# A kernel of mLSTM chunks and a soft mixture of experts on one core: gates, decays and last steps in another order, and the output taken in parts of 128 and 192 columns

## The chip, the cores and the metric

The kernel runs on one core of a Trainium2 chip. The metric is the device time of one execution in microseconds (us). The profile used below is of one execution by the hardware profiler; its own time stands beside the times of the runs without it.

## What is computed

The reference has two parts. The first is a gated recurrence over 768 time steps for 4 batches of 8 heads with 40 features; the second takes its output as 3072 tokens of 320 features.

```python
for t in range(S):
    m_new = np.maximum(f_gate[:, :, t] + m, i_gate[:, :, t])
    f_stab = np.exp(f_gate[:, :, t] + m - m_new)
    i_stab = np.exp(i_gate[:, :, t] - m_new)
    C = f_stab[..., None, None] * C + i_stab[..., None, None] * np.einsum('bhd,bhe->bhde', vt, kt)
    n = f_stab[:, :, None] * n + i_stab[:, :, None] * kt
    y[:, :, t] = sigmoid(o_gate) * (C @ qt) / np.maximum(abs(n @ qt), 1.0)
x = y as (3072, 320)
logits = x @ phi                                  # 32 slots
d = softmax of logits over the tokens             # d.T @ x is the input of the slots
slot_out[e] = relu(slot_input[e] @ w1[e]) @ w2[e] # 8 experts, 4 slots each, width 1024
out = (softmax of logits over the slots) @ slot_out
```

## The kernel before

**The chunks.** The recurrence is cut into 24 steps: chunk c = i // 4 (128 time steps each) of batch i % 4. A step is in matrix form. `expo(i)` (L302) makes a matrix of exponents on PE (tile `pe`) and two exponentials on ACT into a slot of `EWt` (3 slots). `scores(i)` (L340) is the 16 matmuls of keys and queries (`psc`), `mix(i)` (L369) multiplies the two on DVE. `pv(i)` (L411) is the product with the values (`ph`, one buffer). `inter(i)` (L352) is the part that comes from the state, scaled on DVE by `inter_ops` into `itt`; `post1` and `post2` (L424, L441) add it, make the denominator and multiply by the output gate; `gate(i)` (L452) multiplies by the reciprocal into x, on POOL up to step 20 and on DVE in the last steps. `xtr(i)` (L460) transposes x on PE and copies it on ACT. `keys`, `state`, `state_dec` and `state_ops` (L374 to L407) bring the state on: keys scaled on POOL, 16 matmuls into `pst`, decay on POOL, addition on DVE.

**The gates.** `gate_part` (L211) is a chain of scans and elementwise operations on DVE and POOL over a stretch of time: columns 0 to 127 before the loop, 128 to 383 as the list `nxt`, the rest a few at a time in `later`. Its results in `Y` are brought into the operands of `expo` by `side(i)` (ACT, `LLt`) and `spread(i)` (DVE, `RRt`), together `chunk_ops(i)` (L285). `last_sums` and `decays(c)` (L319, L328) make the decays of a chunk: a transpose on PE into the tile `pg`, an exponential on ACT (`eg`), a small matmul into other columns of the same tile, a second exponential (`dS`). `pg` is of the tag `pm`, whose two buffers `pi`, `pt`, `pl`, `pd`, `pc` and `psl` also use in turn. It runs in steps 2, 4, 8, 9 and 10.

**The tokens.** Every 4 steps make a group of 512 tokens: logits (`moe_pl`), a running maximum, the sum over the tokens (`moe_dT`, `moe_psl`, `moe_acc`), and the weights over the slots (`moe_e0`, `moe_e`, `comb_s_ops`, `comb_n`, `comb_hi`, `comb_lo`, `comb_T`, `comb_h`).

**The loop** (L694 to L772) runs steps 1 to 20, with the order of each engine's work as it is written; the last three steps and the last two groups are written out from L775 on. Loads are all issued by SP, in order, and wait there until their buffer is free. In step i it issues `load_kv(i + 2)` and `load_qk(i + 3)`, and weights of the experts (`load_w1`, `load_wave`).

**The end.** `up` is the first matmul of the experts, `relu`, `turn` (transposes), and `down(hf, n, rk)` (L940) the second one, for part hf of the 320 columns; each of its 16 pieces for a part is 4 matmuls in fp32. `gather(hf)` brings a part into `so3`, and `combine(hf, q)` (L962), q from 0 to 11, makes two blocks of 128 tokens for that part of the columns: two matmuls, a copy by DVE (even q) or ACT (odd q) into `ob`, and a store after the q that `STO` names. The pieces of the second part of `down` are spread between the first nine `combine(0, q)` by `PLAN`.

Of the kernel before, what the change touches and what calls it, by code (L numbers as in the profile page):

```python
# [65 lines left out]
HC0 = 192  # L66
PLAN = (3, 0, 0, 3, 0, 0, 3, 0, 3)
QO = (0, 1, 3, 4, 2, 5, 6, 7, 8, 9, 10, 11)
STO = ((1, 4, 2, 6, 8, 9, 11), (1, 5, 9, 11))
# [3 lines left out]
def kernel(ctx: ExitStack, tc: tile.TileContext, qk, kv, og, g0, g1, g2, consts, cb, w1, w2, out):  # L73
# [12 lines left out]
    def ccol(c, n=1):  # L86
        return cst[:, c:c + n]
# [240 lines left out]
    def decays(c):  # L328
        y = g[:, c * L:(c + 1) * L]
        t = pp.tile([P, L + 16], F32, tag="pm", name=f"pg{c}", bufs=2)  # L330
        nc.tensor.transpose(t[:, 0:L], y, ident)
        nc.scalar.activation(eg[:, c].rearrange("p (q a) h -> p q a h", q=2),
                             t[:, 0:L].rearrange("p (q z a l h) -> p q z a l h", q=2, z=2, a=2, l=2)[:, :, 0, :, 0], AF.Exp)
        if c + 1 < NCH:
            nc.tensor.matmul(t[:, L:L + 16], ccol(C_LE, 128), rg.pop(c), start=True, stop=True)
            nc.scalar.activation(dS[:, c].rearrange("p b j -> p (b j)"), t[:, L:L + 16], AF.Exp)
# [357 lines left out]
    for i in range(1, NL - 1):  # L694
# [27 lines left out]
        cmb = i > 2 * GRP - 1 and i % GRP == 0  # L722
        mix(i + 1)
# [22 lines left out]
        if i >= XT:  # L746
            for k in range(0 if i == XT else i - 1, i):
                xtr(k)
        emit(post1_ops(i) + ([lambda: post2(i)] if i > EARLY else []))
        emit(inter_ops(i + 1))  # L750
        if i == 1:
            emit(nxt)
            last_sums(1, CD - 1)
            chunk_ops(4)
# [3 lines left out]
        if i > GRP and i % GRP == 3:  # L758
            emit(comb_s_ops(gi, run["e"]))
            comb_n(run["e"])  # L760
# [26 lines left out]
    gate(i - 1)  # L787
# [6 lines left out]
    emit(inter_ops(NL))  # L794
    inter(NL + 1)
    pl4 = moe_pl(gl - 1, "pm")
    post1(i)
    post2(i)
    pv(NL, pp.tile([P, 2, 512], F32, tag="pe", name="phe")[:, 0])
    mix(NL + 1)  # L800
    emit(inter_ops(NL + 1))
    emit(moe_nm_ops(gl - 1, pl4))
    ex_dT(gl - 1)
    al4 = run["al"]
    ex_lt(gl - 1, pl4)
    xtr(i - 1)
    moe_dT(gl - 1)
    while len(w2_sb) < 9:
        load_wave()
    gate(i)  # L810

    bk = pp.tile([P, 2, 512], F32, tag="psc", name="bk")
    pv(NL + 1, bk[:, 1])
    xtr(i)
    psl4 = pp.tile([P, DM + 1], F32, tag="ph", name="psl4")
    moe_psl(gl - 1, psl4)
    while len(w2_sb) < 16:
        load_wave()
# [9 lines left out]
    gate(NL)  # L828
# [3 lines left out]
    moe_acc(gl - 1, psl4, al4)  # L832
    for h0, h1, kcs in ((0, 4, (0,)), (4, 8, (1, 2))):
        gate(j, None, h0, h1)
        k0, n = kcs[0], len(kcs)
        if h0:
            pt = bk[:, 0, 0:n * P].rearrange("p (k t) -> p k t", k=n)
        else:
            pt = pp.tile([P, n, P], F32, tag="pm", name=f"pt{j}{k0}", bufs=2)
        for kc in kcs:  # L840
            nc.tensor.transpose(pt[:, kc - k0, :], x_of(j)[:, (0, 128, 192)[kc]:(128, 256, 320)[kc]], ident)
        nc.scalar.copy(xT[gl][:, k0:k0 + n, GRP - 1, :], pt)
    pl = bk[:, 1, 0:P]
# [7 lines left out]
    pc3 = comb_T(pc=pq[:, 0].rearrange("p (j t) -> p j t", j=GRP))  # L851
# [18 lines left out]
    nc.tensor.transpose(pd2[0], run["lt"], ident)  # L870
# [113 lines left out]
    comb_h(gl - 2, pc3)  # L984
# [131 lines left out]
```

## Time and profile before

| | |
|---|---|
| median of 3 runs | 190.71 us (188.79 to 194.32) |
| the profiled execution | 188.0 us, of which the span of the trace is 186.2 us |
| granted clock of TensorE, mean over the span | 0.964 |
| busy share PE / DVE / ACT / POOL | 86% / 67% / 46% / 34% |
| read from and written to memory | 42.80 MB and 4.23 MB, 253 GB/s over the span |

PE is TensorE's matmuls, PEld its weight loads, DVE is VectorE, ACT ScalarE, POOL GpSimd, SP the engine that issues the DMAs. Times in the trace count from the start of the span. A row of an instruction that waited has in brackets how long its engine sat idle before it and what released it.

### The profile page before, as it was taken

The numbers are of one execution on the slowest core, as the hardware profiler recorded it, in microseconds if no ns is written. First come the engines' busy times: TensorE is split into PE (matmuls) and PEld (weight loads), VectorE is DVE, ScalarE is ACT, GpSimd is POOL, SyncE is SP. The second block draws the span as 40 slices with busy tenths as digits, with TensorE's granted clock in tenths as the row PEclk, the third lists the DMA queues.
The fourth block names the chain that finished last, engine by engine and source line by source line (L and its number), as shares of the span: only waits on it lengthen the run. The fifth ranks groups of instructions, "written<-read, shape, count | busy, mean of one in ns | idle before, by whom it ended". The sixth has DMA issues, their size and how long they took to land.

```text
span 186.2 us, 6239 instructions
## 1 busy us (share of the span) xinstructions
PE 159.5 (86%) x2594; PEld 117.3 (63%) x2594; DVE 124.1 (67%) x305; ACT 85.8 (46%) x205; POOL 63.1 (34%) x90
## 2 busy tenths in 40 slices
PE   7986657996896989997999989999978798999950
PEld 2554546885586867766877778777764442478740
DVE  6863786279879957479775997779688366323450
ACT  4888643656374544544445336634303432004340
POOL 8038058646336544046434443434211201100000
PEclk9999978999999699999999999999997899999996
DMA  5999998679968899766899989783869998001996
GB/s 173 306 315 367 314 328 279 193 218 376 268 199 271 217 338 302 227 220 175 303 344 293 278 253 364 210 274 100 256 214 364 362 364 267 0 4 57 293 305 194
DMA packets 27323, 47.42 MB, mean 255 GB/s; under 512 B 3184, under 2 KB 18288, under 8 KB 27296
## 3 DMA queue, kind: packets, MB, share of 16 engines
q1 hardware_dynamic: 27296, 47.03, 80.1%
q8 instruction: 20, 0.33, 0.8%
q14 instruction: 7, 0.06, 0.1%
HBM read 42.80 MB, written 4.23 MB: 253 GB/s over the span
## 4 chain that ended last, share of the span: by engine, by line
PE 69%; DVE 13%; ACT 8%; issue 4%; POOL 2%; DVEq 0%; ACTq 0%; POOLq 0%
PE psc L347 11%; PE ph L419 10%; PE pe L309 7%; PE pi L360 6%; PE pt L466 5%; PE pso L945 5%; PE pw L173 4%; DVE EWt L372 3%; PE pst L391 3%; PE po L975 3%; PE bk L917 2%; PE phh L917 2%; DVE RRt L277 2%; PE psl L527 2%; ACT xT L469 2%
## 5 line engine op out<-in xcount | busy, mean ns | idle before, releaser
L456 POOL TENSOR_TENSOR Xt<-sig,den 128x320 f32<-128x320 f32 x20 | 17.1, 856 | 53.1 <-DVE sig L445 53.1
L372 DVE TENSOR_TENSOR EWt<-psc,EWt 128x1024 f32<-128x1024 f32 x24 | 29.2, 1216 | 5.3 <-ACT rl L317 4.6
L347 PE MATMUL psc<-KQt 64*128 64x128 f32 (+1 forms) x384 | 28.6, 290 | 4.0 <-DVE EWt L372 1.9
L469 ACT COPY xT<-pt 128x384 f32<-128x384 f32 x23 | 10.9, 479 | 38.8 <-PE pt L466 38.8
L419 PEld LDWEIGHTS ph<-KVt,EWt 128*64 128x64 f32 x704 | 23.4, 143 | 8.2 <-issue 5.8
L347 PEld LDWEIGHTS psc<-KQt 64*128 64x128 f32 (+1 forms) x384 | 24.1, 192 | 6.4 <-DVE EWt L372 2.8
L311 ACT ACTIVATE EWt<-pe 128x512 f32<-128x512 f32 x48 | 26.0, 593 | 4.6 <-PE pe L309 4.4
L419 PE MATMUL ph<-KVt,EWt 128*64 128x41 f32 x704 | 26.0, 236 | 1.2 <-issue 1.2
L360 PE MATMUL pi<-St,KQt 104*64 104x82 f32 x320 | 15.7, 241 | 0.0
L377 POOL TENSOR_TENSOR KRt<-KVt,rl 128x320 f32<-128x320 f32 x20 | 14.7, 736 | 2.2 <-DMA KVt<-in_kv_dram 1.3
L366 DVE TENSOR_TENSOR itt<-pi,eg 128x328 f32<-128x328 f32 x20 | 10.0, 499 | 6.9 <-PE pi L360 5.7
L360 PEld LDWEIGHTS pi<-St,KQt 104*64 104x64 f32 x320 | 12.5, 136 | 2.3
L391 PE MATMUL pst<-KVt,KRt 128*64 128x41 f32 x160 | 12.8, 230 | 0.8 <-POOL KRt L377 0.7
L466 PE MATMUL pt<-cst,Xt 128*128 128x128 f32 x63 | 11.5, 296 | 2.0 <-DVE itt L366 2.0
L399 POOL TENSOR_TENSOR St<-St,dS 104x328 f32<-104x328 f32 x16 | 12.7, 794 | 0.1
L391 PEld LDWEIGHTS pst<-KVt,KRt 128*64 128x64 f32 x160 | 11.5, 142 | 1.3 <-POOL KRt L377 0.8
L309 PE MATMUL pe<-RRt,LLt 128*64 128x512 f32 (+1 forms) x24 | 9.0, 459 | 3.7 <-DVE RRt L277 2.3
L427 DVE TENSOR_TENSOR ph<-ph,itt 128x328 f32<-128x328 f32 x18 | 9.1, 504 | 3.6 <-PE ph L419 3.6
L591 POOL TENSOR_TENSOR E<-e,E 128x256 fp32r<-128x256 f32 x7 | 5.1, 735 | 14.4 <-ACT E L587 7.8
L393 PE MATMUL pst<-KVt,KRt 128*40 128x41 f32 x160 | 9.9, 207 | 0.0
L445 DVE SCALAR_TENSOR_TENSOR sig<-sig,ph 128x320 f32<-128x320 f32 x22 | 9.6, 438 | 0.0
L466 PEld LDWEIGHTS pt<-cst,Xt 128*128 128x128 f32 x63 | 6.7, 144 | 3.5 <-DVE itt L366 1.2
(227 smaller groups left out, 273.7 us busy)
## 6 DMA issues: line engine op xcount, KB each, us to landing
w<-in_w_dram SPq DMA_DIRECT2D x20, 512.0 KB, 6.2
KVt<-in_kv_dram SPq DMA_DIRECT2D x24, 324.0 KB, 4.7
KQt<-in_qk_dram SPq DMA_DIRECT2D x24, 320.0 KB, 5.5
w<-in_w_dram SPq DMA_DIRECT2D x7, 640.0 KB, 6.9
sig<-in_og_dram SPq DMA_DIRECT2D x6, 640.0 KB
out_dram<-ob SPq DMA_DIRECT2D x5, 384.0 KB, 4.1
KQt<-in_w_dram SPq DMA_DIRECT2D x2, 640.0 KB, 5.3
EWt<-in_w_dram SPq DMA_DIRECT2D x2, 640.0 KB, 9.6
```

The lines of the kernel that those rows point to most:

```text
L309: nc.tensor.matmul(pe[0:x, n], l[0:k, n * LH:n * LH + x], r[0:k, :, n * LH:n * LH + LH], start=True, stop=True)
L311: nc.scalar.activation(w[:, 0:2, :, n * LH:n * LH + LH].rearrange("p e j t -> p j e t"), pe[:, n].rearrange("p (j e) t -> p j e t", e=2), ...
L347: nc.tensor.matmul(psc[:, e, j], t[r0:r1, 1, j], t[r0:r1, 0, j], start=True, stop=True)
L360: nc.tensor.matmul(pi[z, j], q[0:104, 0, j, z], St[0:104, i % B, j], start=True, stop=True, tile_position=(0, 64 * u))
L372: nc.vector.tensor_tensor(w, pscs.pop(i), w, ALU.mult)
L377: e.tensor_tensor(kr[i][:, 24:].rearrange("p (j e d) -> p j e d", e=2, d=D), KV[i % NK][:, 0:DM].rearrange("p (j e d) -> p j e d", e=2, d= ...
L391: nc.tensor.matmul(pst[0:64, j, 0:V1], kr[i][:, h * D:h * D + 64], v_of(i, h), start=True, stop=True)
L399: nc.gpsimd.tensor_tensor(s, s, dS[0:104, i // B, i % B].unsqueeze(2).broadcast_to([104, HP, 2 * V1]), ALU.mult)
L419: nc.tensor.matmul(ph_[z, h * V1:(h + 1) * V1], w[:, h % 2, h // 2, z], v_of(i, h), start=True, stop=True, tile_position=(0, TW * u))
L456: e.tensor_tensor(x_of(i)[:, h0 * D:h1 * D].rearrange("p (h d) -> p h d", d=D), s1_of(i)[:, h0:h1], dens[i][:, h0:h1].unsqueeze(2).broadca ...
L466: nc.tensor.transpose(pt[:, kc, :], x[:, o:o + P], ident)
L469: nc.scalar.copy(xT[i // GRP][:, :, i % GRP, :], pt)
```

## The change

The diff does four things.

- In step 1 the list `nxt` and `last_sums` come ahead of `mix(2)`, and `chunk_ops(4)` ahead of `post1(1)`; before they came after it.
- `decays` writes into columns 328 to 471 of the tile `pst_t` in place of a buffer of `pm`, and issues its small matmul ahead of the first exponential.
- In every fourth step of the loop `comb_n` goes from DVE to POOL. In the last steps `gate` of steps 20, 21 and 22 goes from DVE to POOL; `post1`, `post2` of step 21 come ahead of the second `inter_ops` and `mix`; the logits of group 4 go into `pst_t` and come later, their maximum, exponentials, transposes, token sum and `moe_acc` come after the last `gate`; the transposes and the copy of `comb_T` and `comb_h` for group 3 come ahead of them.
- The first part of the output has 128 columns in place of 192, the second 192 in place of 128. The first part is stored 5 times in place of 7, the second 6 times in place of 4.

```diff
--- before.py
+++ after.py
@@ -63,10 +63,10 @@
 
 DEC = (2, 4, 8, 9, 10)
 
-HC0 = 192
+HC0 = 128
 PLAN = (3, 0, 0, 3, 0, 0, 3, 0, 3)
 QO = (0, 1, 3, 4, 2, 5, 6, 7, 8, 9, 10, 11)
-STO = ((1, 4, 2, 6, 8, 9, 11), (1, 5, 9, 11))
+STO = ((1, 4, 2, 8, 11), (1, 3, 5, 7, 9, 11))
 
 
 @with_exitstack
@@ -327,12 +327,13 @@
 
     def decays(c):
         y = g[:, c * L:(c + 1) * L]
-        t = pp.tile([P, L + 16], F32, tag="pm", name=f"pg{c}", bufs=2)
+        t = pst_t[:, HP * 2 * V1:HP * 2 * V1 + L + 16]
         nc.tensor.transpose(t[:, 0:L], y, ident)
+        if c + 1 < NCH:
+            nc.tensor.matmul(t[:, L:L + 16], ccol(C_LE, 128), rg.pop(c), start=True, stop=True)
         nc.scalar.activation(eg[:, c].rearrange("p (q a) h -> p q a h", q=2),
                              t[:, 0:L].rearrange("p (q z a l h) -> p q z a l h", q=2, z=2, a=2, l=2)[:, :, 0, :, 0], AF.Exp)
         if c + 1 < NCH:
-            nc.tensor.matmul(t[:, L:L + 16], ccol(C_LE, 128), rg.pop(c), start=True, stop=True)
             nc.scalar.activation(dS[:, c].rearrange("p b j -> p (b j)"), t[:, L:L + 16], AF.Exp)
 
     pscs = {}
@@ -720,6 +721,9 @@
         elif 4 < i < NSTEP - GRP and i % GRP == 2:
             sigm(i // GRP + 1)
         cmb = i > 2 * GRP - 1 and i % GRP == 0
+        if i == 1:
+            emit(nxt)
+            last_sums(1, CD - 1)
         mix(i + 1)
         for k in () if i < 2 else (0, 1) if i == 2 else (i - 1,):
             if i == 2:
@@ -746,18 +750,16 @@
         if i >= XT:
             for k in range(0 if i == XT else i - 1, i):
                 xtr(k)
+        if i == 1:
+            chunk_ops(4)
         emit(post1_ops(i) + ([lambda: post2(i)] if i > EARLY else []))
         emit(inter_ops(i + 1))
-        if i == 1:
-            emit(nxt)
-            last_sums(1, CD - 1)
-            chunk_ops(4)
         chunk_ops(i + 4)
         if i > GRP and i % GRP == 2:
             emit(moe_e0_ops(gi, "pm"))
         if i > GRP and i % GRP == 3:
             emit(comb_s_ops(gi, run["e"]))
-            comb_n(run["e"])
+            comb_n(run["e"], nc.gpsimd)
         if i == WRT:
             put_gates()
         if i == WRT:
@@ -784,38 +786,33 @@
     xl.update({i: xy, NL: xr[:, 0], NL + 1: xr[:, 1]})
     expo(NL + 1)
     mix(NL)
-    gate(i - 1)
+    gate(i - 1, nc.gpsimd)
     comb_lo(run["e"])
     nc.gpsimd.memset(xy[:, DM:DM + 1], 1.0)
     nc.gpsimd.memset(xr[:, :, DM:DM + 1], 1.0)
     pv(i)
     scores(NL + 1)
     inter(NL)
-    emit(inter_ops(NL))
-    inter(NL + 1)
-    pl4 = moe_pl(gl - 1, "pm")
     post1(i)
     post2(i)
+    gate(i, nc.gpsimd)
+    mix(NL + 1)
+    emit(inter_ops(NL))
     pv(NL, pp.tile([P, 2, 512], F32, tag="pe", name="phe")[:, 0])
-    mix(NL + 1)
+    inter(NL + 1)
     emit(inter_ops(NL + 1))
-    emit(moe_nm_ops(gl - 1, pl4))
-    ex_dT(gl - 1)
-    al4 = run["al"]
-    ex_lt(gl - 1, pl4)
-    xtr(i - 1)
-    moe_dT(gl - 1)
     while len(w2_sb) < 9:
         load_wave()
-    gate(i)
 
     bk = pp.tile([P, 2, 512], F32, tag="psc", name="bk")
     pv(NL + 1, bk[:, 1])
+    comb_h(gl - 2, comb_T("ph"))
+    while len(w2_sb) < 15:
+        load_wave()
+    pl4 = pst_t[:, HP * 2 * V1:HP * 2 * V1 + P]
+    logits_mm(gl - 1, pl4, range(GRP))
+    xtr(i - 1)
     xtr(i)
-    psl4 = pp.tile([P, DM + 1], F32, tag="ph", name="psl4")
-    moe_psl(gl - 1, psl4)
-    while len(w2_sb) < 16:
-        load_wave()
 
 
     def late(j):
@@ -825,11 +822,10 @@
         emit(ops)
 
     late(NL)
-    gate(NL)
+    gate(NL, nc.gpsimd)
     xtr(NL)
     j = NL + 1
     late(j)
-    moe_acc(gl - 1, psl4, al4)
     for h0, h1, kcs in ((0, 4, (0,)), (4, 8, (1, 2))):
         gate(j, None, h0, h1)
         k0, n = kcs[0], len(kcs)
@@ -840,6 +836,10 @@
         for kc in kcs:
             nc.tensor.transpose(pt[:, kc - k0, :], x_of(j)[:, (0, 128, 192)[kc]:(128, 256, 320)[kc]], ident)
         nc.scalar.copy(xT[gl][:, k0:k0 + n, GRP - 1, :], pt)
+    emit(moe_nm_ops(gl - 1, pl4))
+    ex_dT(gl - 1)
+    al4 = run["al"]
+    ex_lt(gl - 1, pl4)
     pl = bk[:, 1, 0:P]
     logits_mm(gl, pl, [0, 1, 2])
     logits_mm(gl, pl, [3])
@@ -848,7 +848,10 @@
     hx = sb.tile([P, 1024], F32, tag="xT", name="hx")
     hT.extend(hT_of(hx[:, 512 * n:512 * n + 512]) for n in range(2))
     pq = pp.tile([P, 2, 512], F32, tag="pe", name="pq")
-    pc3 = comb_T(pc=pq[:, 0].rearrange("p (j t) -> p j t", j=GRP))
+    moe_dT(gl - 1)
+    psl4 = moe_psl(gl - 1, pp.tile([P, DM + 1], F32, tag="ph", name="psl4"))
+    load_wave()
+    lt4 = run["lt"]
     emit(moe_nm_ops(gl, pl))
     nmf = run["ex"][1]
     ex_dT(gl)
@@ -867,7 +870,8 @@
     for j in range(GRP):
         nc.tensor.matmul(pcol[32 * j:32 * j + 32], row, cst[0:1, C_ONE:C_ONE + 1], start=True, stop=True,
                          tile_position=(0, 32 * j))
-    nc.tensor.transpose(pd2[0], run["lt"], ident)
+    nc.tensor.transpose(pd2[0], lt4, ident)
+    moe_acc(gl - 1, psl4, al4)
     nc.scalar.copy(lt5, pl)
     a = sb.tile([P, 1], F32, tag="a", name="a")
     nM = sb.tile([P, 1], F32, tag="nM", name="nM")
@@ -981,7 +985,6 @@
             run["ob"] = None
 
     up(0, range(1))
-    comb_h(gl - 2, pc3)
     e0 = moe_e0(gl - 1, pd2[0].rearrange("p (j s) -> p j s", j=GRP))
     moe_e(gl - 1, e0)
     comb_s(gl - 1, run["e"])
```

## Rows read from the trace of the kernel before

**Rows 1.** The page: busy time of the engines over the span, the busy share of the 16 DMA engines in 40 equal slices (tenths), and the shares of the chain that ended last by engine:

```profile
PE 159.5 (86%) x2594; PEld 117.3 (63%) x2594; DVE 124.1 (67%) x305; ACT 85.8 (46%) x205; POOL 63.1 (34%) x90
...
DMA  5999998679968899766899989783869998001996
...
PE 69%; DVE 13%; ACT 8%; issue 4%; POOL 2%; DVEq 0%; ACTq 0%; POOLq 0%
```

**Rows 2.** The timeline of steps 0 to 3 (start in us, duration in us, engine, line, operation):

```profile
15.14 1.14 POOL L227 TENSOR_SCALAR gf<-gf,cst 128x256 f32<-128x256 f32 x1
...
17.75 1.23 DVE L372 TENSOR_TENSOR EWt<-psc,EWt 128x1024 f32<-128x1024 f32 x1 [2.98 <-ACT rl L317]
...
20.58 0.64 DVE L228 TENSOR_TENSOR_SCAN g<-rst,gf 128x256 f32<-128x256 f32 x1
...
22.62 1.21 DVE L277 TENSOR_TENSOR RRt<-Y,cst 32x1024 fp32r<-32x1024 f32 x1
...
23.98 0.65 PE L309 MATMUL pe<-RRt,LLt 128*64 128x512 f32 x2 [2.31 <-DVE RRt L277]
...
24.89 0.86 DVE L445 SCALAR_TENSOR_TENSOR sig<-sig,ph 128x320 f32<-128x320 f32 x2
...
25.86 1.94 PE L419 MATMUL ph<-KVt,EWt 128*64 128x41 f32 x32 [1.23 <-issue]
...
33.34 1.13 PE L419 MATMUL ph<-KVt,EWt 128*64 128x41 f32 x32
```

**Rows 3.** Busy time by engine in one stretch (us, then busy time with the count for PE, PEld, DVE, ACT, POOL; granted clock, DMA share, GB/s):

```profile
25.00:30.00 5.00, 4.14 (x64) 3.98 (x64) 4.03 (x8) 1.28 (x4) 3.79 (x4) 0.66 1.05 308
```

**Rows 4.** The timeline of POOL and of the DMA issues in steps 2 to 4, and the DMA issue of 21.75 us with its size and its time to landing in us:

```profile
21.75 0.33 SPq L153 DMA_DIRECT2D KVt<-in_kv_dram  x1
...
KVt<-in_kv_dram SPq DMA_DIRECT2D x1, 324.0 KB, 6.6
...
30.67 0.73 POOL L377 TENSOR_TENSOR KRt<-KVt,rl 128x320 f32<-128x320 f32 x1
...
35.65 0.72 POOL L456 TENSOR_TENSOR Xt<-sig,den 128x320 f32<-128x320 f32 x1 [1.53 <-DVE sig L445]
...
37.97 1.56 POOL L227 TENSOR_SCALAR gf<-gf,cst 128x384 f32<-128x384 f32 x1
```

**Rows 5.** Waits of PE (us in total, times, longest), and the timeline of PE at four of the five `decays`:

```profile
PE pg L335 <- ACT eg L332: 2.3, 4, 0.9
...
32.50 0.39 PE L335 MATMUL pg<-rg,cst 128*128 128x16 f32 x2 [0.92 <-ACT eg L332]
...
67.74 0.39 PE L335 MATMUL pg<-rg,cst 128*128 128x16 f32 x2 [0.56 <-ACT eg L332]
...
74.52 0.40 PE L335 MATMUL pg<-rg,cst 128*128 128x16 f32 x2 [0.49 <-ACT eg L332]
...
80.61 0.33 PE L331 MATMUL pg<-cst,g 128*128 128x128 f32 x1 [0.46 <-ACT xT L469]
```

**Rows 6.** The timeline around `comb_s_ops` and `comb_n` in steps 11, 15 and 19:

```profile
84.99 0.73 POOL L399 TENSOR_TENSOR St<-St,dS 104x328 f32<-104x328 f32 x1
...
85.25 1.19 DVE L575 TENSOR_SCALAR rsum<-rsum 128x4 f32<-128x4 f32 x1
...
86.89 1.22 DVE L372 TENSOR_TENSOR EWt<-psc,EWt 128x1024 f32<-128x1024 f32 x1
...
87.49 0.73 POOL L591 TENSOR_TENSOR E<-e,E 128x256 fp32r<-128x256 f32 x1 [1.08 <-ACT E L587]
...
88.21 1.16 PE L347 MATMUL psc<-KQt 64*128 64x128 f32 x16 [1.10 <-issue]
...
109.34 1.16 PE L347 MATMUL psc<-KQt 64*128 64x128 f32 x16 [0.83 <-PE ph L419]
...
127.78 0.17 DVE L575 TENSOR_SCALAR rsum<-rsum 128x4 f32<-128x4 f32 x1
```

**Rows 7.** The last steps: busy time by engine in one stretch, one group of DVE instructions, and the timeline:

```profile
135.60:145.00 9.40, 7.35 (x125) 4.73 (x119) 8.56 (x25) 2.18 (x7) 0.53 (x1) 0.84 0.94 308
...
L533 DVE SCALAR_TENSOR_TENSOR acc<-acc,al,psl 128x321 f32<-128x321 f32 x1 | 0.6, 551 | 0.2 <-PE psl L527 0.2
...
135.67 0.50 DVE L366 TENSOR_TENSOR itt<-pi,eg 128x328 f32<-128x328 f32 x1 [1.98 <-PE pi L360]
...
142.48 1.30 PE L527 MATMUL psl<-Xt,d 128*32 128x321 f32 x8
...
144.41 0.56 DVE L456 TENSOR_TENSOR w<-sig,den 128x160 f32<-128x160 f32 x2
...
146.09 1.10 PE L474 MATMUL bk<-xT,cst 128*32 128x128 f32 x24 [0.46 <-ACT xT L842]
```

**Rows 8.** The output: two pieces of the chain that ended last, the stores, and busy time by engine in two stretches:

```profile
162.36 1.30 PE pso L945 x32
...
174.43 1.01 PE pso L945 x32
...
170.50 11.07 SPq L980 DMA_DIRECT2D out_dram<-ob  x11
...
173.00:179.00 6.00, 5.97 (x90) 5.21 (x88) 3.93 (x9) 3.34 (x9) 0.00 (x0) 1.00 1.00 321
...
181.00:184.00 3.00, 0.00 (x0) 0.00 (x0) 0.00 (x0) 0.00 (x0) 0.00 (x0) 0.82 1.03 285
```

## The prediction, written before the changed kernel was run

> **What bounds the kernel now.** I read the page first. PE is busy for 86% of the span and makes 69% of the chain that ended last; DVE is the next link with 13%, and the DMA engines run near full load in many slices [rows 1]. So a microsecond is worth something where PE waits, or where a DVE chain runs with PE idle, and the loads may take some of it back. Four places show such waits.
>
> First the start. In the timeline DVE sits idle for 2.98 us ahead of `mix(2)` at 17.75, and only afterwards makes the remaining gate operations (from 20.58) and the spread for step 4 (22.62). `expo(4)` on PE waits 2.31 us for that spread, and `pv(2)` starts at 25.86, right after the two `post2` that DVE began at 24.89 and ended at 25.75 [rows 2]. From 25 to 30 the granted clock is 0.66, that is, part of it at the lower of its two levels, after PE had stood idle before `expo(4)` and again before `pv(2)`; `pv(2)` takes 1.94 us there where `pv(3)` takes 1.13 [rows 2, 3]. Second, `decays`: its small matmul waits for an exponential that does not depend on it, 2.3 us in four steps [rows 5]. Third, in steps 11 and 15 the reductions for `comb_n` sit on DVE ahead of `mix`, and PE's next scores wait 1.10 and 0.83 us [rows 6]. Fourth, the last steps: from 135.60 to 145.00 DVE is busy for 8.56 of 9.40 us, one chain, and the logits of the last group wait for it until 146.09 [rows 7].
>
> **The start, term 1.** POOL ends the operation that the gate list waits for at 16.28 (15.14 + 1.14), within DVE's idle time. The four remaining operations and `last_sums` fill 20.58 to 22.62, 2.04 us, so they run from 16.35 to 18.4 [rows 2]. `mix(2)` slips by 0.65 us, to end at 19.6; what is queued behind it is the spread, and who waits for it is `scores(3)`, which PE reaches at about that time. The cover for this slip is the idle 2.98 us; without it the whole 2.04 us would come back. The spread ends at 20.8, but ACT is in a long operation until about 21.4 and makes its operand after that, so `expo(4)` starts at 22.15 in place of 23.98. DVE then has `post1(1)` (0.6), `mix(3)` and two `post2` (from 23.76 to 25.75 before, 2.0 us): `pv(2)` starts at 23.6, 2.25 us earlier. PE's idle time shrinks from 3.5 us to some 1.2, so I expect the clock to hold: 0.8 us less for `pv(2)` (1.94 against 1.13) and about as much for the scores after it. With the 0.92 us of `decays` in step 2 [rows 5] PE would be 4.7 us earlier at `pv(3)`.
>
> But POOL then sets the pace. The keys of step 4 started at 30.67, and the long gate operation ended at 39.53; of these 8.86 us 1.53 were a wait for `post2(3)`, which now comes early, so 7.33 us remain. The keys need a load issued at 21.75 that landed 6.6 us later, at 28.35 [rows 4]; SP issues it when PE is through with step 1, which does not change. So the gate operation ends at 28.4 + 7.33 = 35.7: **term 1 is -3.8 us**. Bounds: -4.7 where PE alone counts, and -1.0 where the loads behind it land no earlier than now.
>
> **`decays`, term 2.** In step 8 and 9 PE gets back the 0.56 and 0.49 us for which it waited on the exponential, in step 10 the 0.46 us for a buffer of `pm` [rows 5]: **-1.5 us**. In step 4 I count nothing, since there the DVE chain behind the gate scan is late anyway. The two exponentials now read the tile that the state addition on DVE reads too, and if these exclude each other that addition is up to 0.4 us later in one step; DVE has idle time behind it. Bounds: 0 (DVE takes over the pace) and -2.0.
>
> **`comb_n` on POOL, term 3.** DVE is rid of one operation of some 0.2 us (86.68 to the `mix` at 86.89). More is to be had from the operation ahead of it, a tiny one on 128x4: it takes 0.17 us in step 19, where POOL is idle, and 1.19 in step 11, where POOL works from 84.99 on [rows 6]. With `comb_n` in POOL's queue ahead of `gate` of that step, POOL waits for the sums and stands still while DVE makes them, so the tiny operation should take 0.17 there as well. `mix` then starts at about 85.7 in place of 86.89, and both waits of PE (1.10 and 0.83) go: **-1.9 us**. Queued behind the waiting POOL are `gate`, the decay and the keys of the next step, 1.8 us later; PE needs them a step later, over 4 us after. `comb_n` itself on POOL is estimated at 0.45 us, between nothing and the 0.73 us of 87.49 for 256 columns. Bound at the other end: -0.4 (two times 0.2).
>
> The Trainium skill (SBUF — State Buffer, "SBUF: two separate sides") says that DVE and GpSimd share a port pair which one of them holds for a whole instruction, and that the other waits. The 1.19 against 0.17 us agrees with it [rows 6]. It speaks against more work on POOL: by that rule alone, with POOL not standing still, the tiny operation stays at 1.19 us, term 3 is -0.4 and the sum 1.5 us higher.
>
> **The last steps, term 4.** DVE was idle from 133.69, the end of a `gate`, until `inter_ops(22)` at 135.67 (the row's 1.98 us) [rows 7]. Now `post1(21)` starts there, at 133.9, once `pv(21)` is done: 1.75 us. What leaves the chain is `moe_acc` (0.55), two `gate` of half a microsecond, and the maximum of group 4 (0.45), 2.0 us; some 0.5 us of new waits for `inter(23)` come in. The last `gate`, which ended at 144.97, ends at 141.8, and the logits start 3.2 us earlier. POOL does a `gate` in 0.72 [rows 4] against some 0.5 on DVE, with PE's transposes of other steps as cover. Given back: the transposes, the token sum and `moe_acc` of group 4 now stand on the way between the logits and the second matmul. PE waits for the copy of `d` (0.65), the sum takes 0.7 (1.30 at 142.48, at the lower clock), `moe_acc` 0.55 on DVE ahead of a copy that ACT waits for; partly side by side, 0.9 us. What else moves is hidden: the copy for group 3 goes to a time when ACT waits, POOL's zeroing of operands stands behind `gate(22)` and is needed some 6 us later, and SP's loads of the second weights, which wait for the same buffers in another order, end in the last full DMA slice (before 158.3) [rows 1], while `down` starts at 162.36 [rows 8]. **Term 4 is -2.3 us**, between -3.2 and -0.7.
>
> **The output, term 5.** 32 records of `down` take 1.30 us at 192 columns and 1.01 at 128 [rows 8], so the first part is ready 0.9 us earlier (1.1 less a transposing wait), and the second part's pieces cost as much more: the second `gather` stays where it was. What changes is the store queue. From 173 to 179 it moved rows of 768 bytes at 321 GB/s without a pause, and from 181 to 184 rows of 512 bytes at 285 [rows 8]. The first nine blocks now give 1.18 MB in place of 1.77, while PE takes the same 6 us, so the queue runs dry: the store of four blocks is issued at 174.3, the last of part one at 176.6, and it lands at 178.9. Then 2.36 MB remain, 7.3 us at 321 GB/s, to 186.2, against about 184.7 before. **Term 5 is +1.4 us**, between 0 and +2.0.
>
> **The loads, term 6.** The same bytes in less time: the DMA slices from 91 to 113 stand at 9 and 8 already [rows 1]. I take **+0.7 us**, between 0 and +2.5.
>
> **Sum.** -3.8 - 1.5 - 1.9 - 2.3 + 1.4 + 0.7 = -7.4; the profiled execution's 188.0 becomes 180.6. It lies 2.7 us below the median of the runs shown and under the fastest of them (188.79), so for a median I add 1.9, between none and all of it: **182.5 us**, with a range of its own of 178.5 to 186.5.
>
> **The rivals.**
> - **The loads take it back.** The start is earlier but step 4 to 8 wait for keys and values that land when they did, and again in the groups with full DMA slices. For it: 6.6 us from issue to landing at the start, slices at 9. Against it: slices of 6 and 7 in between [rows 1]. Terms 1, 2 and 3 shrink to -1.0, -0.5 and -1.0; with -2.3 and +1.4 the sum is -3.4: 187.3 as a median.
> - **The order does not do what it says.** POOL becomes the link: at the start it is already what sets -3.8, and three more `gate` and `comb_n` stand in its queue. If each takes as long as beside a busy DVE, and the keys come late by it, terms 1 and 3 are nil and term 4 halves: -1.5 - 1.1 + 1.4 = -1.2, or 189.5.
> - **Slower: the store queue decides.** The first part with too few columns starves the stores, and the end is DMA alone. Price: +2.0 of term 5, and 0.4 more as the last store has 393 KB in place of 262. It decides only if the order gives less than 2.4 us, that is, if terms 1 to 4 come to their lower bounds (-1.0, 0, -0.4, -0.7): the sum is then +0.3, 191.0 against the median, and 193.5 with the loads' +2.5. For it: the stores ran without a pause until the end [rows 8].
>
> **Chances.** My forecast 0.58, the loads 0.22, POOL 0.13, slower 0.07. Faster or slower by over 2% (3.8 us, about what a measurement of this kernel can tell from no change) is below 186.9 or above 194.5. The forecast and two fifths of the loads' case lie below: 0.67 with a little off for the forecast's upper edge, say 0.68; slower by that much 0.04; the rest 0.28. The range must leave out no more than 2 in 10: from 178 to 189 it holds the forecast, the loads' case and part of POOL's.
>
> **What would show it.** Term 1: `expo(4)` near 22.2, `pv(2)` near 23.6 at full clock, the gate scan of 39.57 near 35.7. Term 2: the small matmul of `decays` right behind its transpose. Term 3: the 128x4 operation near 0.2 us in steps 11 and 15, and no wait of the scores. Term 4: from the last `mix` to the last logits, 3 us less, and 0.9 us more from there to the first `up`. Term 5: pauses in the stores before the second part, and an end some 1.4 us later after the first `down`. Wrong would be a new wait on kv loads in steps 4 to 8, DVE operations twice as long beside POOL, or a second stretch at the lower clock.

## The result, and the profile after

The changed kernel takes **179.14 us** (median of 4 runs, 178.11 to 179.90) and the kernel before 190.1 us (median of 4 runs beside it): a ratio of **0.944, 95% interval 0.935 to 0.953**, faster. A second measurement (e9 below) gave 179.08 against 192.53 (medians of all runs), ratio 0.948 (0.937 to 0.958); it was judged unclear, and before ran from 187.37 to 197.37 us beside it. The profiled execution of after took 179.9 us with a span of 178.1, against 188.0 and 186.2 before. Runs in which TensorE was throttled more than in others of the same kernel are left out of the ratios, and where too few remain none is given; beside e5 to e8 this was not enough, for twelve of the 13 runs of before there lie 2% or more above its fastest (187.72), so the ratios of e5 and e7 flatter (against that one run their medians give 0.946 and 0.964).

The page of after answers [rows 1]:

```profile
PE 153.0 (86%) x2594; PEld 113.6 (64%) x2594; DVE 119.3 (67%) x298; ACT 84.8 (48%) x205; POOL 66.4 (37%) x97
...
PEclk9999999999999999999999999999999999999985
DMA  5999999999769899997999889994869999105696
...
PE 57%; DMA 14%; DVE 13%; ACT 5%; POOL 3%; issue 3%; SPq 0%; POOLq 0%; DVEq 0%
```

PE is busy 6.5 us less with the same 2594 matmuls, which fits the clock: in this execution after shows the lower level only at the very end. And DMA, which had no share in the chain that ended last, now has 14%. Both come back below.

The timeline of after at the start, beside [rows 2, 4]:

```profile
16.36 0.73 POOL L378 TENSOR_TENSOR KRt<-KVt,rl 128x320 f32<-128x320 f32 x1
...
16.41 1.22 DVE L228 TENSOR_TENSOR_SCAN g<-rst,gf 128x256 f32<-128x256 f32 x1 [1.54 <-POOL gf L227]
...
18.19 0.71 DVE L233 CAST hi_t<-gf 128x256 fp32r<-128x256 f32 x1
...
19.45 1.22 DVE L373 TENSOR_TENSOR EWt<-psc,EWt 128x1024 f32<-128x1024 f32 x1
...
20.58 1.20 DVE L277 TENSOR_TENSOR RRt<-Y,cst 32x1024 fp32r<-32x1024 f32 x1
...
22.40 0.68 PE L309 MATMUL pe<-RRt,LLt 128*64 128x512 f32 x2
...
28.60 1.13 PE L420 MATMUL ph<-KVt,EWt 128*64 128x41 f32 x32
...
35.47 0.74 POOL L378 TENSOR_TENSOR KRt<-KVt,rl 128x320 f32<-128x320 f32 x1 [1.45 <-DMA KVt<-in_kv_dram]
36.18 1.57 POOL L227 TENSOR_SCALAR gf<-gf,cst 128x384 f32<-128x384 f32 x1
36.48 1.16 PE L348 MATMUL psc<-KQt 64*128 64x128 f32 x16 [1.50 <-DMA KQt<-in_qk_dram]
37.78 0.96 DVE L228 TENSOR_TENSOR_SCAN g<-rst,gf 128x384 f32<-128x384 f32 x1 [3.57 <-POOL gf L227]
```

The gate operations now run beside POOL's keys: the scan takes 1.22 us where it took 0.64 [rows 2], so `mix(2)` starts at 19.45 where 18.4 was counted. The waits behind it swallow most of that: `expo(4)` starts at 22.40 (22.15 was predicted), `pv(2)` at 24.31 (23.6) and in 1.13 us, at full clock, and `pv(3)` at 28.60, 4.74 us earlier, the 4.7 that was counted for PE alone. But POOL's keys of step 5 wait 1.45 us for a load of values and keys that has not landed, and the gate scan behind them starts at 37.78, not near 35.7; PE's scores wait 1.50 us for queries at the same time. The chain that ended last shows the load of the keys, and later one of queries (start, duration):

```profile
27.20 8.10 DMA KVt<-in_kv_dram
...
85.08 8.48 DMA KQt<-in_qk_dram
```

The decays of step 4 and of step 8, and the 128x4 operation of step 11 with `comb_n` on POOL, beside [rows 5, 6]:

```profile
39.11 0.27 PE L331 MATMUL pst<-cst,g 128*128 128x128 f32 x1
39.22 0.29 PE L333 MATMUL pst<-rg,cst 128*128 128x16 f32 x2
...
41.29 0.86 PE L475 MATMUL pl<-xT,cst 128*32 128x128 f32 x24 [1.27 <-DVE itt L367]
...
62.48 0.27 PE L331 MATMUL pst<-cst,g 128*128 128x128 f32 x1
62.59 0.29 PE L333 MATMUL pst<-rg,cst 128*128 128x16 f32 x2
...
79.49 0.17 DVE L576 TENSOR_SCALAR rsum<-rsum 128x4 f32<-128x4 f32 x1
...
79.79 1.19 DVE L373 TENSOR_TENSOR EWt<-psc,EWt 128x1024 f32<-128x1024 f32 x1
80.04 0.40 POOL L584 TENSOR_TENSOR e<-e,rsum 128x128 f32<-128x128 f32 x1 [4.47 <-DVE rsum L577]
```

The small matmul stands 0.11 us behind the transpose; the tiny operation takes 0.17 us and `mix` follows at once; POOL stands still for 4.47 us ahead of `comb_n`, which takes 0.40.

The last steps and the stores, beside [rows 7, 8], and busy time by engine in stretches of the output (columns as in [rows 3]):

```profile
136.37 1.10 PE L475 MATMUL bk<-xT,cst 128*32 128x128 f32 x24 [0.46 <-ACT xT L838]
138.09 0.75 PE L528 MATMUL psl<-Xt,d 128*32 128x321 f32 x8 [0.35 <-ACT d L521]
...
152.83 0.62 PE L949 MATMUL pso<-w,KQt 128*32 128x128 f32 x16
...
159.66 14.02 SPq L984 DMA_DIRECT2D out_dram<-ob  x11
```

```profile
160.00:162.00 2.00, 2.00 (x42) 1.47 (x35) 0.76 (x2) 0.37 (x1) 0.00 (x0) 1.00 0.44 133
162.00:164.00 2.00, 2.00 (x40) 1.30 (x32) 0.42 (x1) 0.37 (x1) 0.00 (x0) 1.00 0.69 203
164.00:166.00 2.00, 2.00 (x41) 1.33 (x35) 0.42 (x1) 0.00 (x0) 0.00 (x0) 1.00 0.00 1
166.00:168.00 2.00, 1.82 (x14) 1.62 (x14) 1.27 (x4) 1.38 (x4) 0.00 (x0) 1.00 0.87 261
168.00:176.00 8.00, 2.37 (x18) 1.98 (x16) 2.55 (x6) 2.52 (x6) 0.00 (x0) 0.76 1.01 317
```

From 164 to 166 the DMA engines move 1 GB/s: the store queue is dry, as predicted.

**Where the 8.1 us are.** Each `mix` is one row of the timeline, so the time from one to the next can be compared over all kernels (differences of start times, called gaps below; the profiled execution of each). The first row of before, e2 to e4 and e11 and the last of before and e3 hold stretches at the lower clock:

| from `mix` to `mix` | before | after | e1 start | e2 decays | e3 comb_n | e4 last | e7 after, comb_n on DVE | e11 other loads |
|---|---|---|---|---|---|---|---|---|
| 0 to 6 | 33.96 | 32.08 | 32.77 | 33.88 | 38.11 | 36.72 | 30.41 | 31.79 |
| 7 to 8 | 7.52 | 6.40 | 7.52 | 6.41 | 7.52 | 7.52 | 6.40 | 6.40 |
| 8 to 9 | 5.82 | 4.31 | 5.41 | 5.41 | 4.30 | 5.71 | 5.41 | 4.30 |
| 10 to 11 | 6.49 | 5.67 | 6.50 | 5.68 | 6.50 | 6.50 | 5.66 | 5.66 |
| 11 to 12 | 7.69 | 7.71 | 7.69 | 6.79 | 7.69 | 7.68 | 6.80 | 6.79 |
| 12 to 13 | 6.09 | 4.22 | 6.10 | 5.30 | 4.75 | 6.10 | 5.31 | 4.23 |
| 15 to 16 | 6.63 | 8.44 | 6.80 | 8.18 | 7.16 | 7.68 | 7.27 | 7.00 |
| 16 to 17 | 5.31 | 4.23 | 5.71 | 5.30 | 4.23 | 5.31 | 5.72 | 4.23 |
| 22 to 23 | 5.51 | 3.28 | 5.50 | 5.50 | 5.50 | 3.28 | 3.28 | 3.29 |
| 23 to the last logits | 8.51 | 7.18 | 7.99 | 8.00 | 8.74 | 7.18 | 7.18 | 7.17 |

The last logits to the first `down` take 16.09 us before and 16.46 after, and from there to the end of the span 24.02 and 25.27.

### The profile page after: what moved, and what is told of

It is laid out like the page before. It is cut to its first block, busy times and chain, and to the rows that moved or that the text cites. A ratio compares the mean times of both kernels' runs of the same rounds, so it can differ in the third digit from the quotient of the medians.

```text
span 178.1 us, 6244 instructions
## 1 busy us (share of the span) xinstructions
PE 153.0 (86%) x2594; PEld 113.6 (64%) x2594; DVE 119.3 (67%) x298; ACT 84.8 (48%) x205; POOL 66.4 (37%) x97
## 3 DMA queue, kind: packets, MB, share of 16 engines
HBM read 42.80 MB, written 4.23 MB: 264 GB/s over the span
## 4 chain that ended last, share of the span: by engine, by line
PE 57%; DMA 14%; DVE 13%; ACT 5%; POOL 3%; issue 3%; SPq 0%; POOLq 0%; DVEq 0%
PE psc L348 11%; DMA KQt<-in_qk_dram 8%; PE ph L420 7%; PE pi L361 6%; PE pso L949 5%; DMA KVt<-in_kv_dram 5%; DVE EWt L373 4%; PE pe L309 4%; PE pt L467 3%; PE pst L392 3%; PE bk L921 3%; PE po L979 3%; PE phh L921 3%; DMA cst<-in_consts_dram 2%; DVE RRt L277 2%
## 5 line engine op out<-in xcount | busy, mean ns | idle before, releaser
L348 PE MATMUL psc<-KQt 64*128 64x128 f32 (+1 forms) x384 | 27.9, 285 | 7.7 <-DVE EWt L373 3.3
L348 PEld LDWEIGHTS psc<-KQt 64*128 64x128 f32 (+1 forms) x384 | 23.4, 188 | 10.3 <-DVE EWt L373 4.5
L457 POOL TENSOR_TENSOR Xt<-sig,den 128x320 f32<-128x320 f32 x21 | 17.7, 847 | 28.3 <-DVE sig L446 28.3
L420 PEld LDWEIGHTS ph<-KVt,EWt 128*64 128x64 f32 x704 | 22.3, 138 | 7.9 <-issue 5.2
L420 PE MATMUL ph<-KVt,EWt 128*64 128x41 f32 x704 | 24.9, 232 | 1.2 <-issue 1.2
L392 PE MATMUL pst<-KVt,KRt 128*64 128x41 f32 x160 | 12.3, 226 | 0.9 <-POOL KRt L378 0.7
L309 PE MATMUL pe<-gx 104*64 104x512 bf16 (+1 forms) x24 | 8.7, 396 | 0.0
```

Of the source, the lines that this page charges most:

```text
L309: nc.tensor.matmul(pe[0:x, n], l[0:k, n * LH:n * LH + x], r[0:k, :, n * LH:n * LH + LH], start=True, stop=True)
L348: nc.tensor.matmul(psc[:, e, j], t[r0:r1, 1, j], t[r0:r1, 0, j], start=True, stop=True)
L392: nc.tensor.matmul(pst[0:64, j, 0:V1], kr[i][:, h * D:h * D + 64], v_of(i, h), start=True, stop=True)
L420: nc.tensor.matmul(ph_[z, h * V1:(h + 1) * V1], w[:, h % 2, h // 2, z], v_of(i, h), start=True, stop=True, tile_position=(0, TW * u))
L457: e.tensor_tensor(x_of(i)[:, h0 * D:h1 * D].rearrange("p (h d) -> p h d", d=D), s1_of(i)[:, h0:h1], dens[i][:, h0:h1].unsqueeze(2).broadca ...
```

## The experiments

**e1, the order of step 1 alone** (on the kernel before):

```diff
+        if i == 1:
+            emit(nxt)
+            last_sums(1, CD - 1)
         mix(i + 1)
...
+        if i == 1:
+            chunk_ops(4)
         emit(post1_ops(i) + ...)
         emit(inter_ops(i + 1))
-        if i == 1:
-            emit(nxt)
-            last_sums(1, CD - 1)
-            chunk_ops(4)
```

> The kernel before with the order of step 1 alone changed (gate list, sums and spread ahead). My theory: PE reaches pv(2) near 24.3 and at the higher clock, but the gate scan of step 4 comes only 1.8 us earlier than 39.57, near 37.8, since the keys of step 5 wait for a load; the time falls by 1.8 us (ratio 0.990). Rival, POOL and not the loads sets the scan (the prediction's working): near 35.7, 3.8 us, ratio 0.980. Second rival: the earlier start is lost in the DVE chain of steps 4 to 7, ratio 1.000.

Measured: 189.05 us against 193.54, ratio 0.985 (0.977 to 0.993). Taken alone, e1, and e3 and e4 below, are not clear of the noise at 2%; what each does is read from the gaps. `pv(2)` starts at 24.50, and the clock holds at 1.00 up to 40 us, with 0.85 from 40 to 45. Up to `mix(6)` the profile gains 1.2 us on that of before; the gate scan starts at 38.67, nearer the theory's 37.8 than the rival's 35.7.

**e2, the decays alone** (the tile in `pst_t`, the small matmul ahead of the exponential):

```diff
-        t = pp.tile([P, L + 16], F32, tag="pm", name=f"pg{c}", bufs=2)
+        t = pst_t[:, HP * 2 * V1:HP * 2 * V1 + L + 16]
         nc.tensor.transpose(t[:, 0:L], y, ident)
+        if c + 1 < NCH:
+            nc.tensor.matmul(t[:, L:L + 16], ccol(C_LE, 128), rg.pop(c), start=True, stop=True)
```

> The kernel before with decays alone changed (other tile, small matmul first). Theory: PE gains 0.9 us in step 2, about 0.7 in step 4 and 0.4 in step 5 (a buffer of pm that is free earlier), 0.5 each in steps 8, 9 and 10: the time falls by 2.5 to 3.5 us (ratio 0.984). Rival (the prediction's count): nothing in step 4, 1.5 us from steps 8 to 10 and what is left of step 2, ratio 0.990. Rival: DVE takes over the pace and nothing is left, 1.000.

Measured: 187.94 us (4 runs), no ratio. The table tells more: four gaps shrink, by 1.11, 0.81, 0.90 and 0.79 us, together 3.6, where 1.5 were predicted. The first, from `mix(7)` to `mix(8)`, was in no term. In the gap 15 to 16 the scores then wait 1.49 us for queries, and it grows from 6.63 to 8.18 us.

**e3, `comb_n` on POOL alone:**

```diff
-            comb_n(run["e"])
+            comb_n(run["e"], nc.gpsimd)
```

> The kernel before with comb_n of the loop alone moved from DVE to POOL. Theory (POOL stands still while DVE makes the sums): the 128x4 operation takes 0.17 us in steps 11 and 15 too, both waits of the scores go, the time falls by 1.9 us (ratio 0.990). Rival (only the operation's own 0.2 us leaves DVE): the 128x4 operation stays at 1.2 and 0.7 us, the time falls by 0.4 to 0.7 us (0.997).

Measured: 193.07 us (10 runs) against 193.54, ratio 0.990 (0.981 to 1.000). The 128x4 operation takes 0.17 us in steps 7, 11 and 15, and the gaps 8 to 9, 12 to 13 and 16 to 17 are 1.11 and 1.35 us shorter than in e1, whose clock is 1.00 there too, and 1.08 shorter than before.

**e4, the last steps alone** (their part of the diff, from `gate(i - 1, nc.gpsimd)` on, and `comb_h`):

> The kernel before with the last steps alone changed (gates on POOL, group 4 later). Theory: from the mix of step 22 to the first up 3.2 us less, no other stage changes, ratio 0.983. Rival: the loads of the second weights, which start no earlier relative to the rest, make down wait and take back 1 us or more: ratio 0.989 or above.

Measured: 189.13 us against 193.54, ratio 0.978 (0.963 to 0.994). From `mix(22)` to the first `down` e4 and after both take 26.92 us, e1 29.58, before 30.11. But this profile has more to show. Busy time by engine in stretches of its start, columns as in [rows 3]:

```profile
25.00:30.00 5.00, 3.86 (x48) 3.61 (x48) 4.03 (x9) 1.56 (x4) 3.50 (x4) 0.50 0.99 297
30.00:35.00 5.00, 3.85 (x43) 2.95 (x43) 1.64 (x2) 2.19 (x7) 4.38 (x5) 0.82 0.62 181
35.00:40.00 5.00, 5.00 (x74) 4.67 (x70) 1.06 (x5) 2.46 (x5) 1.25 (x2) 0.52 0.19 75
```

and the same stretches of after:

```profile
25.00:30.00 5.00, 4.73 (x90) 4.04 (x86) 4.02 (x9) 2.33 (x8) 4.18 (x5) 1.00 1.05 321
30.00:35.00 5.00, 4.52 (x85) 3.76 (x85) 2.35 (x5) 3.60 (x8) 3.93 (x5) 1.00 1.04 323
35.00:40.00 5.00, 3.52 (x56) 2.97 (x56) 2.15 (x4) 1.90 (x6) 2.28 (x2) 1.00 0.98 291
```

The start of e4 is that of the kernel before, instruction for instruction, and PE waits there for the same 2.31 and 1.2 us. In the profile of before the clock was at its lower level for part of one stretch [rows 3]; here it is so for most of three, and e4 needs 36.72 us up to `mix(6)` where before needed 33.96. e6, with the same start, shows 0.54, 0.78 and 0.56 and needs 36.64; e3 shows 0.50 in all three and needs 38.11.

**e5, after with the output parts of before:**

```diff
-HC0 = 128
+HC0 = 192
-STO = ((1, 4, 2, 8, 11), (1, 3, 5, 7, 9, 11))
+STO = ((1, 4, 2, 6, 8, 9, 11), (1, 5, 9, 11))
```

> The changed kernel with the output parts of before (192 and 128 columns, 7 and 4 stores): the order alone. Theory: the stores run without a pause again, from the first down to the end 1.3 us less than in the changed kernel, 177.9 us or a ratio of 0.936 to the kernel before. Rival: the pauses cost nothing because the end is set by the last copies, 179.1 us, ratio 0.944.

Measured: 177.55 us against 192.79, ratio 0.914 (0.908 to 0.920). From the first `down` to the end 23.96 us.

**e6, before with the output parts of after** (e5's diff the other way round):

> The kernel before with the output parts alone changed (128 and 192 columns, 5 and 6 stores). Theory: the store queue runs dry in the first part and the end comes 1.3 us later, ratio 1.007. Rival: the first part comes 0.9 us earlier and with it the end, ratio 0.995.

Measured: 194.96 us (10 runs) against 192.79, no ratio. From the first `down` to the end 25.33 us. Over all profiles that stretch is 23.95 to 24.15 us in the nine with 192 columns first (before, e1 to e5, e10 to e12) and 25.27 to 25.72 in the five with 128 (after, e6 to e9).

**e7, after with `comb_n` back on DVE:**

```diff
-            comb_n(run["e"], nc.gpsimd)
+            comb_n(run["e"])
```

> The changed kernel with comb_n of the loop back on DVE. Theory: POOL runs its gate, decay and keys beside the sums again, the 128x4 operation is back at 0.7 to 1.2 us in steps 11 and 15, and the scores wait about 1 us in each; the time rises by 1 to 2 us (ratio 0.951). Rival: the loads that made PE wait in steps 13 to 15 take these 2 us anyway, and the time stays (0.944).

Measured: 181.04 us against 192.79, ratio 0.933 (0.924 to 0.942). The three gaps of e3 grow back, by 1.10, 1.09 and 1.49 us. The rival is right in part: the gaps 11 to 12 and 15 to 16, 7.71 and 8.44 us in after, shrink to 6.80 and 7.27, so that from `mix(6)` to `mix(23)` e7 takes 87.93 us where after takes 86.55. The timeline of step 15 shows how the operation grows back:

```profile
99.96 1.34 DVE L576 TENSOR_SCALAR rsum<-rsum 128x4 f32<-128x4 f32 x1
...
99.85 0.73 POOL L400 TENSOR_TENSOR St<-St,dS 104x328 f32<-104x328 f32 x1
100.54 0.74 POOL L378 TENSOR_TENSOR KRt<-KVt,rl 128x320 f32<-128x320 f32 x1
```

The operation ends at 101.30, when POOL's second row ends (101.28). The Trainium skill (SBUF — State Buffer, "SBUF: two separate sides") has DVE and GpSimd share a port pair, held for a whole instruction; these rows agree. They also fit POOL's next operation going ahead of one of DVE that is already waiting. Moving the work to POOL pays not in spite of that rule but by it: it makes POOL wait at that moment (4.47 us in after), and the operation takes 0.17 us.

**e8, after with the loads of the first weights moved** from steps 0 to 2 to later ones, 6, 7 and 11 above all:

```diff
-W1N = (3,) + 17 * (1,)
+W1N = (1, 0, 0, 1, 1, 1, 2, 2, 1, 1, 1, 2, 1, 1, 1, 1, 1, 1)
```

> The changed kernel with fewer loads of the first expert weights early: 1 in place of 3 ahead of the loop, none in steps 1 and 2, two in steps 6, 7 and 11, the last one behind the loop. Nothing else differs. Theory (in steps 4 and 5 the loads set the pace): the keys of step 5 no longer wait for their load, the gate scan of step 4 starts near 35.8 in place of 37.78, and 1.5 to 2 us of it stay to the end (177.3 us, ratio 0.934). Rival (POOL's own order sets it): the scan stays near 37.8 and the time at 179.1.

Measured: 184.18 us (4 runs), no ratio. The start does what term 1 said, and PE's waits show the price:

```profile
33.26 0.74 POOL L378 TENSOR_TENSOR KRt<-KVt,rl 128x320 f32<-128x320 f32 x1
33.98 1.56 POOL L227 TENSOR_SCALAR gf<-gf,cst 128x384 f32<-128x384 f32 x1
35.58 0.96 DVE L228 TENSOR_TENSOR_SCAN g<-rst,gf 128x384 f32<-128x384 f32 x1 [1.74 <-POOL gf L227]
```

```profile
PE psc L348 <- DMA KQt<-in_qk_dram: 5.2, 2, 2.7
```

The keys of step 5 no longer wait and the scan starts at 35.58 (35.7 was predicted); up to `mix(6)` it takes 29.75 us. Then the scores wait 2.50 and 2.68 us for queries, with the clock falling to a mean of 0.79 from 70 to 75 us and 0.68 from 95 to 100, and the gaps 11 to 12 and 15 to 16 grow to 11.02 and 11.25 us.

e1 to e4 ran on one chip and e5 to e8 on a second. The last four ran on a third: the kernel after and e5 again, and two with loads moved differently, both with 192 columns first.

**e9, the kernel after again.** 

> The changed kernel once more, beside the next three on one chip. Theory of the output (the first part of 128 columns lets the store queue run dry): from the first down to the end of the span 25.3 us, where the order with 192 columns in the first part takes 24.0, so this kernel is 1.3 us slower than the next one. Rival (that difference is the spread of executions): both within 0.5 us of each other.

Measured: 179.08 us, ratio 0.948 (0.937 to 0.958); 25.3 us from the first `down` to the end (151.8 to 177.1). Up to `mix(6)` 30.55 us, 1.5 less than in the first profile of the same kernel.

**e10, e5 again.** 

> The changed kernel with the output parts of before (192 and 128 columns). Theory of the output: 24.0 us from the first down to the end of the span and 1.3 us under the changed kernel. From mix(11) to mix(12) and from mix(15) to mix(16) I expect it to wait for queries as before: 7.3 to 7.7 us and about 8.3 us where 6.8 and 6.6 are without such a wait.

Measured: 178.32 us, ratio 0.942 (0.925 to 0.959); 24.1 us from the first `down` to the end. The stretch is shorter in every profile; the medians of e9 and e10 differ by 0.8 here and the intervals overlap. It waits for queries as expected, but longer in the first gap: 8.77 us from `mix(11)` to `mix(12)` and 7.83 from `mix(15)` to `mix(16)`.

**e11**, on e10: `W1N = (3, 1, 1, 1, 1, 1, 1, 1, 0, 1, 1, 1, 0, 1, 1, 1, 1, 1, 1, 1)`. 

> As the kernel with 192 columns first, and the two loads of first weights of steps 8 and 12 (steps in which the output gates, a second weight and the first weight are all loaded ahead of the next queries) go to steps 18 and 19. Theory (the weight loads hold back the queries of steps 12 and 16, and that is where the order's gain in steps 13 to 15 goes): mix(11) to mix(12) 6.8 us, mix(15) to mix(16) 6.6, the median 2 us lower, at 175.5. Rival (the DMA queues are full as a whole, so a wait only moves): the two gaps shorten but another grows, in steps 18 to 23 above all, and the median stays within 0.7 us.

Measured: 178.50 us, ratio 0.943 (0.932 to 0.954). PE's waits for queries, in e10:

```profile
PE psc L348 <- DMA KQt<-in_qk_dram: 4.3, 3, 1.9
```

In e11 PE waits for queries once, 0.58 us at 37.25, and no longer in these two gaps; they are 6.79 and 7.00 us (6.6 was expected for the second), and from `mix(6)` to `mix(23)` it takes 84.20 us where e10 takes 86.99, e5 85.99 and after 86.55. So the cause of these waits is shown. The median did not follow, though (175.5 was expected), so the rival holds for the time as a whole; where the other executions lose as much again no profile shows.

**e12**, on e10: `W1N = (1, 1, 1, 1, 1, 1, 1, 1, 0, 1, 1, 1, 0, 1, 1, 1, 1, 1, 2, 1, 1)`. 

> As the one before, and two of the three first weights that are loaded ahead of step 1 go to steps 18 to 20 as well. Theory of term 1 (the keys of step 5 wait for values and keys that land behind weight loads): the gate scan of step 4 starts at 35.6 us in place of 37.3 and the median is 1.5 us lower still, at 174. Rival (it comes back later, as it did where four of these loads were only moved to steps 6, 7 and 11): the scan at 35.6, but the median at that of the kernel before it in this list or higher.

Measured: 181.32 us (175.35 to 183.63), no ratio. The scan starts at 36.79 (35.6 was expected), since its keys still wait 0.50 us for their load, and from `mix(21)` on the time comes back: scores wait once more, and the clock falls.

```profile
121.95 1.36 PE L348 MATMUL psc<-KQt 64*128 64x128 f32 x16 [1.60 <-DVE sig L446]
```

```profile
120.00:125.00 5.00, 3.40 (x47) 2.91 (x44) 2.16 (x7) 0.87 (x2) 2.30 (x6) 0.78 1.04 274
125.00:130.00 5.00, 5.00 (x53) 3.72 (x51) 2.65 (x7) 1.56 (x3) 0.00 (x0) 0.50 0.74 252
```

PE's busy time is full from 125 to 130 at half the clock. No version with other loads has a lower median than e5's order (177.55, and 178.32 in e10), though e11's 178.50 can't be told from it and the fastest single run is one of e12 (175.35).

## Why the prediction was right, and where its steps were not

182.5 was forecast as a median and 180.6 for the profiled execution; measured were 179.14 and 179.9. The sum held because errors of both signs cancel, so that 180.6 came so close is luck in part. Two of the prediction's own signs of being wrong appeared: a new wait on a load of keys and values (1.45 us), and a DVE operation twice as long beside POOL (the scan, 1.22 against 0.64). By the table:

| term | predicted | in the profile of after |
|---|---|---|
| 1, the start (`mix` 0 to 6) | -3.8 | -1.9 |
| 2, decays (7 to 8, and 10 to 13) | -1.5 | -3.6 |
| 3, `comb_n` | -1.9 | -3.1 |
| gap 8 to 9, before against e1 | none | -0.4 |
| 4, the last steps | -2.3 | -3.2 |
| 5, the output | +1.4 | +1.25 |
| 6, the loads (11 to 12, 15 to 16) | +0.7 | +2.7 |

Their sum is -8.25; with +0.1 at the first `mix` and the rounding it is the -8.1 between the spans.

**Term 1** went wrong at "the keys need a load issued at 21.75": that is the load for the keys of step 4. The next one, for step 5, was left out, and since PE and DVE now come earlier it lands after POOL is ready (8.10 us in the chain). e8 settles it: with fewer weight loads ahead the scan starts at 35.58 and the start gains 4.2 us. So the mechanism was right, and the rival of the loads took half of the term in this execution; in e9 and e7, where the same keys wait only 0.79 and 0.64 us, the gain is 3.4 and 3.6.

**What the prediction missed about the start** is in the kernel before. It took the 0.66 of one stretch [rows 3] as the price of PE's idle time and added 1.9 us, up to the median of the runs shown, as if that were the same for both kernels. e3, e4 and e6 show the same waits (2.31 us, then 1.10 to 1.24) followed by 0.50 to 0.82 over 15 us, 2.7 to 4.2 us more up to `mix(6)`. Under the old order of the start the clock falls in every profile taken (before, e2 to e4, e6), and how long it stays down differs; under the new one after, e1, e5, e7, e8, e9 and e12 stay at 1.00 from 25 to 40, and e10 and e11, where it dips too (a mean of 0.66 and 0.71 from 20 to 25), are back at 0.95 or more from 25 to 35 (e10 dips again, to 0.84 and 0.82 up to 45). After's median lies at its profile (179.14 and 179.9), while the medians of before, 190.1 to 193.5, lie 2 to 6 us above its own. That this is the clock behind the start fits e1's gain in the medians of all runs (4.5 us; 2.9 by the ratio) against 1.2 in the profiles up to `mix(6)`, but it is inferred, not measured apart. The clocks over whole executions say that the start alone is not enough: 0.897 to 0.963 in the 13 runs of before beside e1, 0.946 to 0.953 in three of e1's four, 0.982 to 0.988 in the first four of after, and 0.944 in one run of e9, which took 186.94 us. Where the other falls lie no profile of those runs shows.

**Term 2.** "In step 4 I count nothing, since there the DVE chain behind the gate scan is late anyway" failed. In before PE's `pg` of step 4 waits 1.25 us for `itt`, which frees the buffer of `pm` that it needs, and a step later the transposes wait for the next `itt`:

```profile
43.08 0.33 PE L331 MATMUL pg<-cst,g 128*128 128x128 f32 x1 [1.25 <-DVE itt L366]
...
46.37 1.16 PE L347 MATMUL psc<-KQt 64*128 64x128 f32 x16
...
49.84 0.52 PE L466 MATMUL pt<-cst,Xt 128*128 128x128 f32 x3 [0.88 <-DVE itt L366]
```

In after the transpose of `decays` runs at 39.11 right behind the transposes of x, and although PE waits again at 41.29, it keeps a part of the lead: the next scores start 1.26 us after `mix(6)` (1.95 in before), and `pv(6)` 6.05 us after it (7.01). The gap 7 to 8 cashes it: 1.1 us in every kernel with the new decays and in none without. The three steps that were counted gave 0.8 to 0.9 each rather than 0.5: removing a wait that the row shows with 0.56 us also removes the drained start of what follows, which is my reading of the difference; the runs show only its size.

**Term 3.** The mechanism is as predicted and e3 and e7 bracket it from both sides. The failed part is the count: `comb_s_ops` runs in step 7 too, where the operation took 1.22 us before, and the prediction counted only steps 11 and 15:

```profile
61.18 1.22 DVE L575 TENSOR_SCALAR rsum<-rsum 128x4 f32<-128x4 f32 x1
```

Against e1, where it takes 0.68 us, step 7 gives 1.1 us; step 11 gives 1.1 on top of the decays, step 15 1.1, with 0.3 from step 19 and 0.2 given back behind each of three. The 0.4 by which before's gap 8 to 9 exceeds e1's belongs here too: the operation is 0.54 us longer and `comb_n` 0.24 shorter, `itt` starts 0.12 later (the clock is 0.63 from 59 to 63 us), and `mix` follows DVE's chain without a wait. The rule of the Trainium skill (SBUF — State Buffer, "SBUF: two separate sides") that spoke against it would have left 0.4 by the prediction's count; POOL's standing still decided.

**Term 4.** The `gate` that ends at 133.69 is that of step 20; before, POOL made them only up to step 19. The logits of the last group are 3.56 us earlier after `mix(22)`, and 0.37 are given back where 0.9 were counted. Of the total of 3.2, 0.5 is the lower clock that before shows from 142 to 145 us and e1 does not (30.11 against 29.58); the order itself gives 2.7 (29.58 to 26.92). Which of its moves gives how much was not tried apart.

**Term 5** came as predicted, queue run dry and all; the parts of before with the new order are 1.3 us shorter in the trace. So this part of the change costs time, and the rest pays for it.

**Term 6** was the worst sized: 2.7 us in two gaps, besides the start. The scores' wait for queries is shown by the rows of the second gap in after (1.39 us) and by those of the first in e9 and e10 (1.76 and 1.90). Terms 2 and 3 bring it with them, since PE now asks for the queries earlier: e2 shows the second wait with the decays alone, and without term 3 (e7) both gaps are shorter by 0.9 and 1.2 us, so that of its 3.1 us 1.4 are left from `mix(6)` to `mix(23)`. The prediction went by DMA slices; what counted was which load stands ahead of which. In steps 8 and 12 output gates (640 KB), a second weight (640) and a first weight (512) are issued ahead of the next queries; without that first weight (e11) the waits of these two gaps are gone.

## What to carry to other kernels

A wait removed early is worth what the next resource lets through: follow the load behind the one that was named, for the step after. PE's idle time can cost more than its length where the lower clock follows it (here 2.7 to 4.2 us between executions with the same waits), and one profile does not show how much; take several executions of the kernel before. And count a mechanism in every iteration whose condition holds, not only in the first ones found.

## What the runs showed of the hardware

- The same instructions with the same waits were followed by a lower clock for part of one 5 us stretch in one execution (before) and for most of three in another (e4): 0.66, 1.00, 1.00 against 0.50, 0.82, 0.52.
- A DVE operation on 128x4 took 0.17 us with POOL at rest and up to 1.34 beside it, and in e7 it ended within 0.02 us of POOL's second operation.
- A scan of 128x256 took 0.64 us with POOL at rest [rows 2] and 1.22 in after, where it started 0.05 us after POOL's keys; the cast after it took 0.71 us beside the next keys and 0.29 in before.
- Moving two loads (e11) took the waits for queries out of two gaps and 1.8 to 2.4 us out of the steps from `mix(6)` to `mix(23)` (against e5 and after), and the median stayed where it was.
